# Attention with a norm, then a gated convolution FFN: the norm factor of two batches carried to all lanes by transfers through DRAM

## The chip, the cores and the metric

The kernel runs on one core of one Trainium2 chip. A core has a matrix engine (PE, with its weight loads shown apart as PEld), a vector engine (DVE), a scalar engine (ACT), a general engine (POOL) and a queue engine (SP) that here does nothing but issue transfers. Matmul results land in eight banks of an on-chip accumulator memory (`banks` in the program); everything else that the engines touch lies in SBUF, on 128 partitions ("lanes"). The inputs and the output lie in DRAM. Each engine works its own instructions strictly in order; engines wait for each other, and for transfers, on semaphores. The metric is the device time of one execution in microseconds (us), lower is better.

## The reference

```python
kv  = einsum('bhsd,bhse->bhde', k, v)          # 8 batches, 8 heads, 576 rows, 64 columns
o   = einsum('bhsd,bhde->bhse', q, kv)
rms = sqrt(mean(o * o, axis=-1) + 1e-6)        # over the 64 columns of one head and row
x   = o / rms * g_norm                         # heads side by side: [8, 576, 512]
h   = maximum(x @ w_in, 0)                     # [8, 576, 1024]
c   = conv over rows, 3 taps, one weight per column and tap
out = (h * sigmoid(c)) @ w_out                 # [8, 576, 512]
```

The part of interest is the factor 1/rms. There is one number per batch, head and row, and it multiplies the 64 columns of that head.

## The kernel before

Everything is computed transposed: the 512 columns of `x` lie on the partitions, as four tiles of 128 (two heads to a tile), and the 576 rows lie along the free axis. Work on a batch is cut by `u` (tiles 0 and 1, or 2 and 3) and by `s` (two parts of the rows; for batches 6 and 7 these are 320 and 256 columns wide). A piece is called (b, u, s) below.

The whole program is one long written order, the string `ORDER` (lines 59 to 135). Each token is an operation, its arguments, and after `@` the slots of the buffers that it takes; lines 779 to 784 run the tokens, and lines 786 to 794 chain every engine's instructions in exactly that order. So nothing is rescheduled: an engine that has to wait holds up all that stands behind it on that engine, and SP's transfers are issued in the order of their tokens.

For batches 4 and 5 together, and again for 6 and 7 together, the norm is done so:

- `ox` (L491) makes a piece of `o` in two banks; `oc` (L518) copies it to SBUF as `o32` in fp32, and `sq` (L506) squares it, both on ACT.
- `ss` (L560) sums the squares over the 64 columns with PE, against a 0/1 matrix `sel`. The sums of both batches end in one bank, one sum to a lane: lane 32 t + 2 c + i holds tile t, head i of that tile, and c = 2 (b - b0) + s.
- `ln` (L571) turns them into factors on ACT: `rs`, 128 lanes by 320 columns, fp32 (its activation is L574).
- `sl` (L577) splits `rs` on DVE into bf16 parts `wparts` (four instructions, L581 to L584). Each factor lies on three lanes, and each lane keeps another part (high, middle, low).
- `sp` (L587) spreads a factor over the 64 lanes of its head: two matmuls for each piece against the 0/1 matrix `spread` (L593), which add the three parts up again in fp32 in two banks.
- `mu` (L598) multiplies on DVE: `x = o32 * g * spread factor`, one instruction for each piece (L599).

Then `hs` (L624, matmuls L628; one half of the rows of one tile f of `h`) and `hm` (L608, L613; a whole batch) make `h` from `x` and `w_in`. `rh` and `re` (L633, L618) apply the relu on ACT. `ta`, `aa`, `ab` (L678 to L692) make the convolution on DVE, `sg` (L695) the sigmoid on ACT, `mg` (L720) the gate product on DVE. `om` (L727, L732) is the product with `w_out`, four tiles f at a time; `ea` and `ed` (ACT, DVE) copy its result to SBUF, and `st` (L746, transfer L748) issues the store from SP.

Around the change the order is this. `ln.6`, then on DVE `sl.6`, then six pieces: `mu.6.1.1`, `mu.6.0.1`, `mu.7.0.0`, `mu.7.1.0`, `mu.7.1.1`, `mu.7.0.1`; behind them `mg.4.2.2`, the convolution of two tiles of batches 4 and 5, `mg.4.2.3`, and then `mu.6.0.0` and `mu.6.1.0`. PE has the six `sp` in two groups around the eight matmuls of `om.1.5`, then the eight of `om.1.3`, then `hs.7.6.0`, which reads (7, 0, 0) and (7, 1, 0), then `hs.7.6.1`, which reads (7, 1, 1) and (7, 0, 1), and from there `hs` and `hm` without another product to put between. The last two `sp` stand about 7 us further on. On SP there are the stores `st.1.2` and `st.0.5` in this stretch, then `st.1.3` and `st.1.1`.

Of the kernel before, what the change touches and what calls it, by code (L numbers as in the profile page):

```python
# [109 lines left out]
sq.7.0.0@3 om.1.2.4.4 ea.1.2@1 om.1.8.4.4 ea.1.8@3 ox.7.1.1@6 sq.7.1.1@4 ox.7.0.1@0 sq.7.0.1@5 ox.7.1.0@2 sq.7.1.0@7  # L110
oc.7.0.1@7 om.1.1.0.4@4 om.1.1.4.4 ss.6.6.2@5 ss.7.6.2 ln.6@0 oc.7.1.1@2 st.1.0 st.1.8 ea.1.1@4 oc.7.1.0@3
om.1.4.0.4@0 om.1.4.4.4 ea.1.4@2 om.1.7.0.4@1 ta.4.2.7@1 ta.4.2.6 aa.4.2.3 ab.4.2.3 om.1.7.4.4 ea.1.7@3 ta.4.2.5
aa.4.2.2 ab.4.2.2 sg.4.2.4 sg.4.2.5 sg.4.2.7 sl.6@1 sp.6.1.1.6@6 mu.6.1.1@0 sp.6.0.1.6@4 mu.6.0.1 sp.7.0.0.6@2
mu.7.0.0@2 st.1.2 st.0.5 om.1.5.0.4@0 om.1.5.4.4 sp.7.1.0.6@6 mu.7.1.0 sp.7.0.1.6@4 sp.7.1.1.6@2 om.1.3.0.4@1
om.1.3.4.4 ea.1.3@1 st.1.3 st.1.1 hs.7.6.0@6 rh.7.6.0@1 mu.7.1.1 mu.7.0.1 hs.7.6.1@7 hs.7.4.0@2 hs.7.2.1@1 rh.7.4.0
rh.7.6.1 rh.7.2.1 hs.7.5.0@3 rh.7.5.0 ea.1.5@0 sg.4.2.6 hs.6.7.1@2 rh.6.7.1 hm.4.2@4 hs.6.0.1@3 rh.6.0.1 hs.6.6.1@0
rh.6.6.1 re.4.2 hm.4.3@6 re.4.3 hs.7.0.0@1 mg.4.2.2 hs.7.1.1@0 rh.7.1.1 ta.4.2.1@0 ta.4.2.0 aa.4.2.0 mg.4.2.3 ab.4.2.0
sg.4.2.0 sp.6.0.0.6@2 mu.6.0.0 sp.6.1.0.6@4 mu.6.1.0 hs.7.2.0@6 rh.7.2.0 sg.4.2.1 hs.7.3.0@0 hs.7.5.1@7 rh.7.3.0
ta.4.2.3@1 ta.4.2.2 aa.4.2.1 ab.4.2.1 rh.7.0.0 mg.4.2.0 st.1.5 hs.6.3.1@2 hs.6.2.1@3 hs.6.4.0@6 hs.6.7.0@4 rh.6.4.0
rh.6.7.0 hs.6.4.1@0 rh.6.4.1 hs.6.3.0@1 rh.6.3.1 rh.6.3.0 hs.6.1.1@5 rh.6.1.1 rh.6.2.1 hs.6.5.1@0 rh.6.5.1 ta.6.1.4@0  # L120
hs.6.6.0@2 rh.6.6.0 hs.6.5.0@1 rh.6.5.0 ta.6.1.5 hs.6.0.0@3 aa.6.1.2 sg.4.2.2 hs.7.4.1@0 hs.7.7.1@1 sg.4.2.3 rh.7.7.1
# [17 lines left out]
def kernel(  # L139
# [20 lines left out]
    NT = D_model // P  # L160
# [71 lines left out]
    GW = 320 if TQ else HS  # L232
    HEAD = (("sync", "q.0.0 k.0.1 k.1.1 q.1.0 k.2.1 k.3.1 q.0.1 q.1.1"), ("scalar", "v.0.2 v.2.2"))

    def cols(b, s):
        if b == 0:
            return tuple(r * D for r in RS[s])
        if b in TQ:
            return s * 5 * D, (5 + s * 4) * D
        return s * HS, (s + 1) * HS  # L240

    def width(b, s):
        c0, c1 = cols(b, s)
        return c1 - c0

    @op
    def pre():
        T["stg"] = ring("h", [P, 2, NT, R * D], FP32, "stg")
        T["stq"] = ring("h", [P, NT, R * D], FP32, "stq")
        for name, head in HEAD:  # L250
            queue = getattr(nc, name)
            for what in head.split():
                x, t, s = what.split(".")
                t, s = int(t), int(s)
                if x == "q":
# [9 lines left out]
        nc.vector.memset(zero, 0.0)
# [92 lines left out]
    @op  # L358
    def Li(f0, n):
        at = slice(f0 * P, (f0 + n) * P)  # L360
        nc.gpsimd.dma_start(out=w_in_sb[:, :, at], in_=moe_w_in[:, at].rearrange("(t p) f -> p t f", p=P))

    @op
    def Lo(f0, n):
# [41 lines left out]
                            start=(r == 0), stop=(r == R - 1))  # L406

    def kvc(eng, b, u0, n):
        if u0 == 0:
            T["kvb", b] = ring("kvb", [P, 2, 2 * D], BF16, "kvb")  # L410
        at = slice(u0 * D, (u0 + n) * D)
        to, fr = T["kvb", b][:, :, at], T["kv", b, u0][:, :, at]
        if eng:
            nc.vector.tensor_copy(to, fr)
        else:
            nc.scalar.activation(to, fr, AX.Copy)

    @op
    def kva(b, u0, n): kvc(0, b, u0, n)

    @op
    def kvd(b, u0, n): kvc(1, b, u0, n)
# [12 lines left out]
                        qkv["q", b][half(i), 2 * u + tt, r * D:(r + 1) * D], ident[half(i), half(i)])  # L435

    def qc(eng, b, u, s):
        if s == 0:
            T["qT", b, u] = ring("qT", [P, 2, S], BF16, "qT")
        c0, c1 = cols(b, s) if b == 0 else (0, S)  # L440
        to, fr = T["qT", b, u][:, :, c0:c1], T["qt", b, u, s][:, :, c0:c1]
        if eng:
            nc.vector.tensor_copy(to, fr)  # L443
        else:
            nc.scalar.activation(to, fr, AX.Copy)

# [150 lines left out]
    @op  # L597
    def mu(b, u, s):  # L598
        nc.vector.scalar_tensor_tensor(  # L599
            x_part(b, u, s), T["o32", b, u, s], g_sb, T["sp", b, u, s], op0=AL.mult, op1=AL.mult)  # L600
# [178 lines left out]
    for token in ORDER.split():  # L779
        what, _, at = token.partition("@")  # L780
# [44 lines left out]
```

## Time and profile before

| | |
|---|---|
| Time, median of 3 runs | 177.79 us (177.78 to 178.52) |
| Span of the profiled execution | 175.6 us, 5070 instructions |
| PE busy | 167.9 us (96%) |
| DVE busy | 149.5 us (85%) |
| ACT busy | 148.9 us (85%) |
| Mean transfer rate over the span | 166 GB/s |

The profile is of one execution, and its times start at the first instruction. The times of the runs take in a little more than that span: 177.79 against 175.6 us, 2.2 us. The views used below are: the page's summary; the chain of work that ended last, in order of time; the timeline of one engine, in which a row is a run of like instructions (start, duration of the whole run, engine, line, operation, output <- inputs, shapes, count, and in brackets the idle time ahead of it with what ended it); the answer about one line or a group of transfers, with the time from issue to landing; and a table of stretches of time with the busy time of each engine in each. "SPq" rows are the issue of a transfer, not the transfer itself. Matmuls overlap in their pipeline, so the duration of one matmul (some 0.3 us) is not its spacing.

### The profile page before, as it was taken

To read this page: it belongs to the slowest core of one execution; us is meant where nothing else is said; L and a number is where in the kernel's file an instruction comes from. 1 tells how busy PE (TensorE), PEld (TensorE's weight loads), DVE (VectorE), ACT (ScalarE), POOL (GpSimd) and SP (SyncE) were. 2 spreads that over 40 slices of the span, in tenths; PEclk is the share of its full clock that TensorE was granted. 3 is DMA by queue.
4 is the path that set the end of the run, shared out by engine and by line. 5 is a ranking of instruction groups with operands and counts; after the bars stand their busy time and mean duration, and the time that the engine had idled before them with its cause. 6 is when DMAs were issued, how large, how long until landed. Compare 5 with 4: busy or idle time off the path is not lost.

```text
span 175.6 us, 5070 instructions
## 1 busy us (share of the span) xinstructions
PE 167.9 (96%) x2097; PEld 100.0 (57%) x2114; DVE 149.5 (85%) x290; ACT 148.9 (85%) x268; POOL 22.2 (13%) x35
## 2 busy tenths in 40 slices
PE   7979999999999999999999999999999999999992
PEld 2334766676447677644467764444877744444451
DVE  2796638899688899999999998989999999999950
ACT  2368899999978999999999998999999967676721
POOL 3094512200603013030000000000000000000000
PEclk9999999999999999999999999999999999999999
DMA  5999999999999999999999050330310003064486
GB/s 159 392 323 207 207 207 207 208 208 209 207 241 230 227 207 207 170 182 197 258 181 161 14 134 0 119 123 0 119 63 0 0 0 116 13 239 175 179 304 237
DMA packets 25911, 29.11 MB, mean 166 GB/s; under 512 B 6036, under 2 KB 20384, under 8 KB 25888
## 3 DMA queue, kind: packets, MB, share of 16 engines
q0 software_dynamic: 13296, 14.50, 49.2%
q1 hardware_dynamic: 12048, 13.11, 26.2%
q10 hardware_dynamic: 544, 1.18, 1.7%
q8 instruction: 16, 0.26, 0.6%
q14 instruction: 7, 0.06, 0.1%
HBM read 32.52 MB, written 9.44 MB: 239 GB/s over the span
## 4 chain that ended last, share of the span: by engine, by line
PE 76%; DVE 12%; ACT 5%; DMA 3%; issue 3%; ACTq 0%; DVEq 0%
PE banks L732 32%; PE banks L628 14%; PE banks L613 9%; PE banks L658 4%; DMA stg<-in_v_dram 3%; PE banks L460 3%; DVE h L722 2%; PE banks L708 2%; ACT taps L698 2%; PE banks L402 2%; PE banks L593 2%; PE banks L433 1%; PE banks L528 1%; DVE taps L681 1%; PE banks L286 1%
## 5 line engine op out<-in xcount | busy, mean ns | idle before, releaser
L732 PE MATMUL banks<-w_out_sb,h 128*128 128x512 bf16 x267 | 62.8, 379 | 1.2 <-issue 0.6
L698 ACT ACTIVATE taps<-taps,cw 128x576 bf16<-128x576 bf16 (+1 forms) x44 | 40.6, 958 | 5.7 <-DVE taps L692 5.5
L732 PEld LDWEIGHTS <-h 128*128 128x128 bf16 x280 | 26.2, 98 | 30.0 <-issue 1.1
L628 PE MATMUL banks<-x,w_in_sb 128*128 128x288 bf16 (+2 forms) x256 | 34.2, 286 | 0.0
L640 ACT ACTIVATE h<-banks 128x288 bf16<-128x288 f32 (+2 forms) x80 | 29.5, 460 | 0.3 <-PE banks L658 0.2
L628 PEld LDWEIGHTS <-w_in_sb 128*128 128x128 bf16 x256 | 24.4, 98 | 7.8 <-issue 0.8
L722 DVE TENSOR_TENSOR h<-h,taps 128x1152 bf16<-128x1152 bf16 (+1 forms) x24 | 22.8, 952 | 1.2 <-ACT taps L698 1.2
L687 DVE TENSOR_TENSOR taps<-taps 128x1152 bf16<-128x1152 bf16 (+1 forms) x22 | 21.5, 978 | 0.5
L509 ACT ACTIVATE sq<-banks 128x576 bf16<-128x576 f32 (+2 forms) x32 | 20.8, 691 | 1.1 <-PE banks L460 1.1
L692 DVE TENSOR_TENSOR taps<-taps,h 128x1152 bf16<-128x1152 bf16 (+1 forms) x22 | 21.4, 972 | 0.3
L681 DVE TENSOR_SCALAR taps<-h,cw 128x576 bf16<-128x576 bf16 (+1 forms) x44 | 18.7, 424 | 0.6 <-ACT h L665 0.5
L682 DVE TENSOR_SCALAR taps<-h,cw 128x576 bf16<-128x576 bf16 (+1 forms) x44 | 18.4, 418 | 0.0
L738 ACT ACTIVATE row<-banks 128x512 f32<-128x512 f32 x23 | 13.5, 597 | 5.7 <-PE banks L732 4.2
L658 PE MATMUL banks<-x,w_in_sb 128*128 128x288 bf16 (+2 forms) x128 | 17.7, 286 | 0.1
L613 PE MATMUL banks<-x,w_in_sb 128*128 128x288 bf16 x128 | 16.9, 286 | 0.0
L556 DVE SCALAR_TENSOR_TENSOR x<-banks,cw,rs 128x576 bf16<-128x576 f32 (+2 forms) x16 | 13.0, 816 | 3.9 <-ACT rs L545 3.6
L658 PEld LDWEIGHTS <-w_in_sb 128*128 128x128 bf16 x128 | 12.0, 98 | 4.4 <-issue 0.5
L227 ACT ACT_TABLE_LOAD x10 | 12.8, 1283 | 2.0 <-issue 1.8
L613 PEld LDWEIGHTS <-w_in_sb 128*128 128x128 bf16 x128 | 12.3, 98 | 3.7 <-issue 0.2
L443 DVE COPY qT<-banks 128x1152 bf16<-128x1152 bf16 (+2 forms) x13 | 8.8, 681 | 5.7 <-PE banks L433 5.7
L545 ACT ACTIVATE rs<-banks,eps_sb 128x576 f32<-128x576 f32 (+2 forms) x16 | 11.8, 740 | 1.1 <-PE banks L528 1.1
L599 DVE SCALAR_TENSOR_TENSOR x<-o,cw,banks 128x576 bf16<-128x576 f32 (+2 forms) x16 | 12.1, 810 | 0.7 <-PE banks L593 0.5
(89 smaller groups left out, 162.9 us busy)
## 6 DMA issues: line engine op xcount, KB each, us to landing
out_dram<-row SPq DMA_DIRECT2D x35, 256.0 KB, 2.3
q_sb<-in_q_dram POOLq DMA_DIRECT2D x6, 576.0 KB, 17.9
k_sb<-in_k_dram POOLq DMA_DIRECT2D x6, 576.0 KB, 14.5
v_sb<-in_v_dram POOLq DMA_DIRECT2D x6, 576.0 KB, 17.9
stg<-in_v_dram ACTq DMA_DIRECT2D x2, 576.0 KB, 6.2
stg<-in_k_dram SPq DMA_DIRECT2D x4, 288.0 KB, 6.9
w_in_sb<-in_moe_w_in_dram POOLq DMA_DIRECT2D x2, 512.0 KB, 9.9
w_out_sb<-in_moe_w_out_dram POOLq DMA_DIRECT2D x1, 1024.0 KB, 15.5
```

The costliest lines, as they stand in the source:

```text
L509: nc.scalar.activation(T["sq", b, u, s], T["o", b, u, s], AX.Square)
L613: nc.tensor.matmul(ps[:, s, :HS], w_in_sb[:, t, f * P:(f + 1) * P], T["x", b][:, t, c0:c1], start=(t == 0), stop=(t == NT - 1))
L628: nc.tensor.matmul(ps, w_in_sb[:, t, f * P:(f + 1) * P], T["x", b][:, t, c0:c1], start=(t == 0), stop=(t == NT - 1))
L640: nc.scalar.activation(h, fr, AX.Relu)
L658: nc.tensor.matmul(T[at], w_in_sb[:, t, f * P:(f + 1) * P], T["x", b][:, t, c0:c1], start=(t == 0), stop=(t == NT - 1))
L681: nc.vector.tensor_scalar_mul(tap[:, 0, f % 2, :n, 8:8 + S], h[:, f], cw[:, f:f + 1])
L682: nc.vector.tensor_scalar_mul(tap[:, 1, f % 2, :n, :S], h[:, f], cw[:, 2 * NF + f:2 * NF + f + 1])
L687: nc.vector.tensor_add(tap[:, 1, :, :n, :S], tap[:, 0, :, :n, 7:7 + S], tap[:, 1, :, :n, 1:1 + S])
L692: nc.vector.tensor_add(y, y, span(b, n)[:, 2 * j:2 * j + 2])
L698: nc.scalar.activation(y, y, AX.Sigmoid, scale=cw[:, NF + f:NF + f + 1])
L722: nc.vector.tensor_mul(h, h, tap_of(b, j)[:, 1, :, :n, :S])
L732: nc.tensor.matmul(T["om", p, m], h[:, f, m * P:(m + 1) * P], w_out_sb[:, f, :], start=(f == 0), stop=(f == NF - 1))
```

## The change

For batches 6 and 7 alone, `sl.6` and the eight `sp` are taken out. In the place of `sl.6` stands `dw.6`: SP writes `rs` (128 lanes by 320 columns, fp32, 164 KB) to a scratch tensor `rd` in DRAM. In the place of each `sp` stands a `df`: two transfers from SP, one to each half of the lanes, which read two rows of `rd` (one factor row for each tile of the piece) and write each of them to 64 lanes. The target is an fp32 tile `spread` in SBUF, laid into buffers that held `q`, `k` or `v` of earlier batches. `mu` is the same instruction; it reads the factor from SBUF now, not from the banks. The places in the order are the same, and batches 4 and 5 keep the split and the products.

So SP issues 17 transfers more: one, then six (for three pieces), then, behind `st.1.2` and `st.0.5`, six more, and, behind `st.1.3` and `st.1.1`, four. PE has 16 matmuls and 16 weight loads fewer, DVE four instructions fewer. The buffer `k` slot 0 is used twice, for (6, 0, 1) and then for (7, 1, 1), so the second transfer waits for `mu.6.0.1`.

The diff also defines operations for loading `w_in` in another way (`w` in `pre`, `wd`, `wa`), and lets `kvc` and `qc` make their tile at any first call; the order uses none of that.

```diff
-aa.4.2.2 ab.4.2.2 sg.4.2.4 sg.4.2.5 sg.4.2.7 sl.6@1 sp.6.1.1.6@6 mu.6.1.1@0 sp.6.0.1.6@4 mu.6.0.1 sp.7.0.0.6@2
-mu.7.0.0@2 st.1.2 st.0.5 om.1.5.0.4@0 om.1.5.4.4 sp.7.1.0.6@6 mu.7.1.0 sp.7.0.1.6@4 sp.7.1.1.6@2 om.1.3.0.4@1
+aa.4.2.2 ab.4.2.2 sg.4.2.4 sg.4.2.5 sg.4.2.7 dw.6 df.6.1.1.6@1 mu.6.1.1@0 df.6.0.1.6@0 mu.6.0.1 df.7.0.0.6@1
+mu.7.0.0@2 st.1.2 st.0.5 om.1.5.0.4@0 om.1.5.4.4 df.7.1.0.6@2 mu.7.1.0 df.7.0.1.6@1 df.7.1.1.6@0 om.1.3.0.4@1
 om.1.3.4.4 ea.1.3@1 st.1.3 st.1.1 hs.7.6.0@6 rh.7.6.0@1 mu.7.1.1 mu.7.0.1 hs.7.6.1@7 hs.7.4.0@2 hs.7.2.1@1 rh.7.4.0
 rh.7.6.1 rh.7.2.1 hs.7.5.0@3 rh.7.5.0 ea.1.5@0 sg.4.2.6 hs.6.7.1@2 rh.6.7.1 hm.4.2@4 hs.6.0.1@3 rh.6.0.1 hs.6.6.1@0
 rh.6.6.1 re.4.2 hm.4.3@6 re.4.3 hs.7.0.0@1 mg.4.2.2 hs.7.1.1@0 rh.7.1.1 ta.4.2.1@0 ta.4.2.0 aa.4.2.0 mg.4.2.3 ab.4.2.0
-sg.4.2.0 sp.6.0.0.6@2 mu.6.0.0 sp.6.1.0.6@4 mu.6.1.0 hs.7.2.0@6 rh.7.2.0 sg.4.2.1 hs.7.3.0@0 hs.7.5.1@7 rh.7.3.0
+sg.4.2.0 df.6.0.0.6@0 mu.6.0.0 df.6.1.0.6@0 mu.6.1.0 hs.7.2.0@6 rh.7.2.0 sg.4.2.1 hs.7.3.0@0 hs.7.5.1@7 rh.7.3.0
...
+    dram = pool("dram", 1, space=bass.MemoryType.DRAM)
...
+    @op
+    def dw(b0):
+        T["rd", b0] = dram.tile([P, GW], FP32, name="rd")
+        nc.sync.dma_start(out=T["rd", b0], in_=T["rs", b0])
+
+    @op
+    def df(b, u, s, b0):
+        w, c = width(b, s), 2 * (b - b0) + s
+        to = T["sp", b, u, s] = ring("qkv"[(4 * (b - b0) + 2 * u + s) % 3], [P, 2, 320], FP32, "spread")[:, :, :w]
+        fr = T["rd", b0].rearrange("(t c i) w -> c i t w", t=NT, i=2)[c, :, 2 * u:2 * u + 2, :w]
+        for i in range(2):
+            nc.sync.dma_start(out=to[half(i)], in_=fr[i].unsqueeze(0).to_broadcast([D, 2, w]))
```

More of the change, by code (lines that the diff above doesn't have):

```diff
@@ L244, in width @@
         return c1 - c0
+    w_rows = moe_w_in.rearrange("(t p) f -> p t f", p=P)
     @op
@@ L254, in pre @@
                 t, s = int(t), int(s)
-                if x == "q":
+                if x == "w":
+                    T["stw", t] = ring("x", [P, NT, s * P], FP32, "stw")
+                    queue.dma_start(out=T["stw", t], in_=w_rows[:, :, t * P:(t + s) * P])
+                elif x == "q":
                     ts, (c0, c1) = slice(2 * t, 2 * t + 2), cols(0, s)
@@ L360, in Li, with wd, wa @@
         at = slice(f0 * P, (f0 + n) * P)
-        nc.gpsimd.dma_start(out=w_in_sb[:, :, at], in_=moe_w_in[:, at].rearrange("(t p) f -> p t f", p=P))
+        nc.gpsimd.dma_start(out=w_in_sb[:, :, at], in_=w_rows[:, :, at])
+    @op
+    def wd(f0, n):
+        nc.vector.tensor_copy(w_in_sb[:, :, f0 * P:(f0 + n) * P], T["stw", f0])
+    @op
+    def wa(f0, n):
+        nc.scalar.activation(w_in_sb[:, :, f0 * P:(f0 + n) * P], T["stw", f0], AX.Copy)
     @op
@@ L408, in kvc @@
     def kvc(eng, b, u0, n):
-        if u0 == 0:
+        if ("kvb", b) not in T:
             T["kvb", b] = ring("kvb", [P, 2, 2 * D], BF16, "kvb")
@@ L437, in qc @@
     def qc(eng, b, u, s):
-        if s == 0:
+        if ("qT", b, u) not in T:
             T["qT", b, u] = ring("qT", [P, 2, S], BF16, "qT")
@@ L600, in mu @@
             x_part(b, u, s), T["o32", b, u, s], g_sb, T["sp", b, u, s], op0=AL.mult, op1=AL.mult)
+    @op
+    def dw(b0):
+        T["rd", b0] = dram.tile([P, GW], FP32, name="rd")
+        nc.sync.dma_start(out=T["rd", b0], in_=T["rs", b0])
+    @op
+    def df(b, u, s, b0):
[4 more added lines that the diff above has]
+            nc.sync.dma_start(out=to[half(i)], in_=fr[i].unsqueeze(0).to_broadcast([D, 2, w]))
     def h_of(b, f):
```

## The prediction

> **What bounds the kernel now.** I read the page's summary first, then the chain that ended last, then stretches, then the timelines of PE and DVE around the change, and SP's last.
>
> ```profile
> span 175.6 us, 5070 instructions
> GB/s 159 392 323 207 207 207 207 208 208 209 207 241 230 227 207 207 170 182 197 258 181 161 14 134 0 119 123 0 119 63 0 0 0 116 13 239 175 179 304 237
> PE 76%; DVE 12%; ACT 5%; DMA 3%; issue 3%; ACTq 0%; DVEq 0%
> ```
>
> The chain is PE for 76% of the span. An average hides where, so here is the chain in order of time (start, duration, what), from the change on:
>
> ```profile
> 118.22 0.34 PE banks L593 x4
> 119.28 1.54 DVE x L599 x2
> 120.86 0.28 PE banks L593 x2
> ...
> 122.98 2.94 PE banks L628 x24
> ...
> 129.98 11.11 PE banks L628 x88
> ...
> 141.35 10.74 PE banks L732 x49
> ...
> 172.27 0.38 ACT row L767
> ```
>
> From 122.98 to 172.27 the chain is matmuls, with no wait that another engine ends: 24 in 2.94 us is 0.1225 us each, 49 in 10.74 is 0.219 each. PE has no room there, so a delay of PE at 123 us comes out at the end. Only the stretch before shows another engine (two `mu`). The stretches (us of the stretch, then busy of PE, PEld, DVE, ACT, POOL, granted clock, DMA share, GB/s):
>
> ```profile
> 118.00:123.00 5.00, 4.82 (x31) 1.96 (x31) 4.55 (x8) 4.97 (x6) 0.00 (x0) 1.00 0.00 0
> 130.00:140.00 10.00, 10.00 (x81) 7.80 (x82) 9.90 (x16) 9.94 (x21) 0.00 (x0) 1.00 0.01 2
> ```
>
> DVE is full as well (9.90 of 10.00), so a delay of DVE is not caught up either. No bytes move from 118 to 123: the new transfers have the queues to themselves.
>
> **The change: what goes.** PE, then DVE, then the activation that makes `rs`, then two single `mu`:
>
> ```profile
> 118.22 0.42 PE L593 MATMUL banks<-wparts,spread 32*128 32x256 bf16 x6
> 118.58 1.90 PE L732 MATMUL banks<-w_out_sb,h 128*128 128x512 bf16 x8
> 120.41 0.74 PE L593 MATMUL banks<-wparts,spread 32*128 32x320 bf16 x6
> 121.08 1.90 PE L732 MATMUL banks<-w_out_sb,h 128*128 128x512 bf16 x8
> 122.82 3.10 PE L628 MATMUL banks<-x,w_in_sb 128*128 128x320 bf16 x24
> 129.67 0.31 PE L593 MATMUL banks<-wparts,spread 32*128 32x320 bf16 x4
> ...
> 114.66 1.36 DVE L692 TENSOR_TENSOR taps<-taps,h 128x2304 bf16<-128x2304 bf16 x1
> 116.30 0.33 DVE L581 CAST hi<-rs 128x320 bf16<-128x320 f32 x1 [0.28 <-ACT rs L574]
> 117.61 0.55 DVE L584 SCALAR_TENSOR_TENSOR wparts<-hi,nb,rs 128x320 bf16<-128x320 bf16 x1
> 118.61 4.35 DVE L599 SCALAR_TENSOR_TENSOR x<-o,cw,banks 128x512 bf16<-128x512 f32 x6 [0.45 <-PE banks L593]
> 122.88 1.35 DVE L722 TENSOR_TENSOR h<-h,taps 128x2304 bf16<-128x2304 bf16 x1
> 127.67 1.36 DVE L722 TENSOR_TENSOR h<-h,taps 128x2304 bf16<-128x2304 bf16 x1 [0.32 <-ACT taps L698]
> ...
> 115.74 0.53 ACT L574 ACTIVATE rs<-banks,eps_sb 128x320 f32<-128x320 f32 x1
> ...
> 120.76 0.88 DVE L599 SCALAR_TENSOR_TENSOR x<-o,cw,banks 128x640 bf16<-128x640 f32 x1
> ...
> 122.22 0.74 DVE L599 SCALAR_TENSOR_TENSOR x<-o,cw,banks 128x512 bf16<-128x512 f32 x1
> ```
>
> PE loses the 16 `sp` matmuls: 118.58 - 118.22 = 0.36, 121.08 - 120.41 = 0.67, and 0.3 at 129.67; 1.3 us. The first two let `om.1.5` and `om.1.3` run earlier, so PE is through them at 122.82 - 1.03 = 121.8. DVE loses `sl.6`, 116.30 to 118.16, 1.9 us, but it gains nothing by that: `mu` is next and now waits for transfers. `mu` keeps its price: the factor comes from SBUF in place of the banks, and `sl`'s instruction of the same kind with both inputs in SBUF takes 0.55 us for 320 columns against 0.74 for 512, so I see no discount (bounds: 0.1 us either way for each, 0.6 in six).
>
> **What comes, on SP.** No row shows a transfer that reads DRAM into 64 lanes. The nearest: `kvx` (64 lanes, SBUF to SBUF), the stores (SBUF to DRAM), and the first loads:
>
> ```profile
> 99.23 0.46 SPq L489 DMA_DIRECT2D kvx<-kvb  x1
> ...
> 99.74 0.59 SPq L489 DMA_DIRECT2D kvx<-kvb  x1
> ...
> 100.38 0.58 SPq L748 DMA_DIRECT2D out_dram<-row  x1
> ...
> DMA to landing us min/median/max: 1.8/1.8/1.9
> ...
> 124.24 0.33 SPq L748 DMA_DIRECT2D out_dram<-row  x1
> ...
> 124.61 0.43 SPq L748 DMA_DIRECT2D out_dram<-row  x1
> ...
> DMA to landing us min/median/max: 1.9/2.2/2.5
> ...
> stq<-in_q_dram SPq DMA_DIRECT2D x2, 256.0 KB, 5.7
> ```
>
> The first landing row is of the two `kvx` at 99 us, the second of the two 128 KB stores at the end. Issues on SP follow one another: 99.23, 99.74, 100.38 is one each 0.5 to 0.64 us, the two stores one each 0.38 to 0.48. I take 0.6 for a `df` transfer (nearest in shape), with 0.42 and 0.65 as ends, and 0.85 for `st.1.2` with `st.0.5`. For issue to landing I take 2.0 (ends 1.75 and 3; the 5.7 of the first loads was beside a rate of up to 392 GB/s). A pair writes 128 lanes x 2 rows x 256 or 320 fp32 numbers; six pairs carry 4 x 262 + 2 x 328 KB = 1.70 MB in the some 8 us of their issue; at the 207 GB/s of the long load phase that takes 8.2 us, so bandwidth is about even with the issues and I add nothing.
>
> - `rs` is there at 115.74 + 0.53 = 116.27. `dw.6` issues at 116.3 and lands at 118.3. Everything behind it on SP waits, stores included; they have time.
> - `df` number k (0 to 11) issues at 118.35 + 0.6 k, plus 0.85 from k = 6 on. A pair is there 2.0 us after its second issue: 120.95 for (6,1,1), 122.15 for (6,0,1), 123.35 for (7,0,0), 125.4 for (7,1,0), 126.6 for (7,0,1), 127.8 for (7,1,1). The last pair's buffer is free long before, after `mu.6.0.1` at 122.9.
> - DVE is free from 116.02 and stands until 120.95, then runs each `mu` as its pair lands. `mu.7.1.0` ends at 125.4 + 0.05 + 0.88 = 126.3, `mu.7.1.1` starts at 127.85, `mu.7.0.1` 0.7 later (six in 4.35 us before) and ends at 129.3. Before it ended at 122.22 + 0.74 = 122.96: DVE is 6.3 us late.
> - PE stands from 121.8 to 126.3, does `hs.7.6.0` (four matmuls of 320 columns, 0.54 us by 0.1225 for a mean of 288), and stands again until 129.3 for `hs.7.6.1`, which before started at 122.82 + 0.54 = 123.36: PE is 5.94 late, and 5.64 after the 0.3 of the last two `sp`.
> - The last four `df`, behind two more stores, issue by 129 and land by 131; `mu.6.0.0` stands at 130.2 + 6 on DVE. Nothing: the queue on DVE covers them, with 5 us to spare.
> - ACT meanwhile has its sigmoids and copies; `sg.4.2.6` behind PE's `hs.7.5.0` slides with PE, so `mg.4.2.3` moves from 127.67 by the larger of PE's 5.94 and DVE's 6.3 - 0.32: 5.97 late.
>
> At the end the two delays meet again (DVE's last gate product, and the matmuls in the window of its first reader; `om.3.7.4.4` is the second of the two, at 166.82):
>
> ```profile
> 165.91 0.75 DVE L722 TENSOR_TENSOR h<-h,taps 128x1152 bf16<-128x1152 bf16 x1
> ...
> 166.61 0.59 PE L732 MATMUL banks<-w_out_sb,h 128*128 128x512 bf16 x2
> ```
>
> The product ends at 166.66, 0.16 us ahead of its reader. So the end is late by the larger of 5.64 and 5.97 - 0.16 = 5.8. Span 175.6 + 5.8 = 181.4; with the 2.2 us around it (the median 177.79 less the span) 183.6.
>
> The Trainium skill ("DMA: Bandwidth & Descriptors", Anatomy of one DMA) gives a transfer about 2.0 us fixed, most of it waiting for the write to be confirmed, plus its bytes at 436 GB/s. It speaks against this change, which puts two such waits in a row where 2.3 us of split and product stood. By it `dw` and each `df` land after 2.0 + 0.4 us, 0.8 later in all, and the time would be 184.4. The rows of this trace (1.9 to 2.5 us for 128 KB) agree as far as they go; that fit is for the other way of issuing.
>
> **The rivals.**
>
> *The stall also halves the PE clock.* The first fillers ran slow and the next fast, and the idle tail kept the full clock:
>
> ```profile
> 1.20 4.45 PE L286 MATMUL banks<-zero 128*128 128x512 bf16 x10 [1.20 <-DVE zero L265]
> 5.83 2.12 PE L286 MATMUL banks<-zero 128*128 128x512 bf16 x9
> ...
> 172.30:175.60 3.30, 0.00 (x0) 0.00 (x0) 0.00 (x0) 0.36 (x1) 0.00 (x0) 1.00 0.53 188
> ```
>
> Ten matmuls took 4.45 us from idle; at the later 2.12 / 9 they would take 2.36, so a cold start costs 2.1 us. Against: 3.3 us of idle at the end left the granted clock at 1.00. For: here PE stands 4.5 us, works 0.5, and stands 2.4 more. PE late by 5.64 + 2.1, and DVE by about as much through `sg.4.2.6`: 185.6. The Trainium skill ("TensorE: Matmul & The Clock Gate", Part 1) says that an idle window of about 3.4 us, free-running, drops the clock to half, and a busy one brings it back; by that rule the 4.5 us hold a whole window in one third of the phases, more if the 0.5 us between count as idle. The trace bears it out at the start only.
>
> *The transfers are slower than their issue.* Each reads two rows of at most 1280 bytes 64 times over; no row shows such reads. At half of 207 GB/s the 1.70 MB take 16.4 us, 8 more than I allow, and the time would be 191. Against: nothing else moves then.
>
> *Not slower.* The round trip fits into what stood there. For that `mu.7.0.1` must be through by 123.36 + 0.3, so the last pair must land by 122.3, its second issue be out by 120.3, 1.95 us after the first: 0.15 us for each of the 13 steps from issue to issue, two stores among them. The shortest issue row is 0.33. If it did fit, the 1.3 us of PE are left and the time would be 176.5.
>
> **How the numbers follow.** Stall with the clock kept, 183.6: 0.50. Stall with half clock, 185.6: 0.27. Slow transfers, 187 to 193: 0.13. A shorter chain (issues at 0.42, landings at 1.75, `dw` at 1.9: the last `mu` at 126.9, PE 3.6 late, 181.4, less with cheaper `mu`): 0.06. Not slower: 0.04, half of it a gain. With the last few of the slow ones and the last case left out the range is 180.9 to 188.5; the likeliest case alone has 181.4 to 185. About 0.5% (0.9 us) can be told from no change. Slower 0.96, same 0.02, faster 0.02.
>
> **What would show it.** DVE idle from 116.0 to about 121 before the first `mu`, ended by a transfer, and gaps of 0.5 us and more between the six; PE idle about 4.5 and 2.4 us ahead of and behind one `hs`; SP issuing `df` each 0.6 us; the last `mu` of the six at about 129.3; the end 5.8 late with no new idle of PE behind 130. The forecast is wrong if a `df` pair takes far other than 2.6 us from its first issue, if the granted clock drops after the stall, or if PE shows idle ahead of `om` at the end.

## The result and the profile after

| | before | after |
|---|---|---|
| Time, median | 177.81 us | 188.88 us |
| Ratio | | 1.062 (95%: 1.060 to 1.064) |
| Span of the profiled execution | 175.6 us | 187.0 us |
| PE busy, share of the span | 96% | 91% |
| Mean granted clock of PE | 1.00 | 0.973 |

The kernel is 11.1 us slower. The forecast was 183.6 us with a range up to 188.5: the sign was right, the size was not, and the time lies 0.4 us outside the range. Two lines of the page's slices show the place (40 slices of 4.7 us each; busy tenths of PE, then the granted clock in tenths):

```profile
PE   7889999999999999999999999912599999999992
PEclk9999999999999999999999999995589999999999
```

One hole in PE, at slices 27 to 29, and from its second slice on three with a lower clock (0.5, 0.5 and 0.8). The rest is as full as before. The timeline of DVE, the six `mu` (L613):

```profile
122.55 0.75 DVE L613 SCALAR_TENSOR_TENSOR x<-o,cw,spread 128x512 bf16<-128x512 f32 x1 [6.45 <-DMA spread<-rd]
124.58 0.75 DVE L613 SCALAR_TENSOR_TENSOR x<-o,cw,spread 128x512 bf16<-128x512 f32 x1 [1.29 <-DMA spread<-rd]
125.89 0.88 DVE L613 SCALAR_TENSOR_TENSOR x<-o,cw,spread 128x640 bf16<-128x640 f32 x1 [0.55 <-DMA spread<-rd]
128.92 0.88 DVE L613 SCALAR_TENSOR_TENSOR x<-o,cw,spread 128x640 bf16<-128x640 f32 x1 [2.15 <-DMA spread<-rd]
131.40 1.41 DVE L613 SCALAR_TENSOR_TENSOR x<-o,cw,spread 128x512 bf16<-128x512 f32 x2 [1.59 <-DMA spread<-rd]
```

Each `mu` is held by a transfer, and the last of the six ends at 131.40 + 1.41 = 132.81; the forecast had 129.3. PE's timeline (L759 is `om`, L655 `hs`):

```profile
118.46 3.61 PE L759 MATMUL banks<-w_out_sb,h 128*128 128x512 bf16 x16 [0.18 <-ACT row L765]
126.83 0.65 PE L655 MATMUL banks<-x,w_in_sb 128*128 128x320 bf16 x2 [4.75 <-DVE x L613]
129.86 0.69 PE L655 MATMUL banks<-x,w_in_sb 128*128 128x320 bf16 x2 [2.39 <-DVE x L613]
132.87 4.64 PE L655 MATMUL banks<-x,w_in_sb 128*128 128x256 bf16 x20 [2.32 <-DVE x L613]
```

PE stands three times (4.75, 2.39 and 2.32 us), not twice: `hs.7.6.0` reads two pieces, so its matmuls fall into two pairs. `hs.7.6.1` starts at 132.87 against 123.36 before (by the prediction's working), 9.5 us late; less the 0.3 us of the last two `sp` that is 9.2. Then 20 matmuls take 4.64 us, 0.23 each, where the forecast went by 0.1225: another 2 us. Together 11.2, and 177.8 + 11.2 = 189.0 is the time to 0.1 us. The chain of the last-ending work and the stretches confirm that nothing more was lost behind it:

```profile
116.38 1.76 DMA rd<-rs
...
121.76 4.01 DMA spread<-rd
...
127.18 4.13 DMA spread<-rd
...
152.43 29.35 PE banks L759 x136
```

```profile
123.00:130.00 7.00, 0.79 (x3) 0.35 (x3) 2.81 (x4) 1.42 (x2) 0.00 (x0) 0.78 0.77 244
130.00:140.00 10.00, 7.68 (x45) 5.21 (x44) 6.75 (x9) 4.93 (x11) 0.00 (x0) 0.64 0.55 151
140.00:150.00 10.00, 9.96 (x82) 7.76 (x81) 9.93 (x15) 9.68 (x21) 0.00 (x0) 1.00 0.01 2
```

In the chain, transfers stand where two `mu` stood, and three of them come to 9.9 us; `om` at the end starts at 152.43, 11.1 us later than the 141.35 of before. In the stretches (columns as before) PE works 0.79 of 7 us between 123 and 130, the clock is 0.64 between 130 and 140, and from 140 to 150 PE is full at full clock; the chain behind that is PE's matmuls up to the last copy.

### The profile page after: what moved, and what is told of

Its sections match the earlier page's. It is cut to its first block, busy times and chain, and to the rows that moved or that the text cites. A ratio compares the mean times of both kernels' runs of the same rounds, so it can differ in the third digit from the quotient of the medians.

```text
span 187.0 us, 5080 instructions
## 1 busy us (share of the span) xinstructions
PE 170.7 (91%) x2098; PEld 100.6 (54%) x2098; DVE 147.9 (79%) x286; ACT 149.2 (80%) x268; POOL 22.2 (12%) x35
## 4 chain that ended last, share of the span: by engine, by line
PE 79%; DMA 8%; DVE 5%; ACT 3%; SPq 2%; issue 1%; DVEq 0%; ACTq 0%
PE banks L759 28%; PE banks L655 18%; PE banks L640 9%; PE banks L685 7%; DMA spread<-rd 4%; DMA stg<-in_v_dram 3%; PE banks L474 3%; PE banks L447 2%; PE banks L416 2%; SPq L627 2%; PE banks L292 2%; PE banks L735 2%; PE banks L542 2%; PE banks L607 1%; PE banks L784 1%
## 5 line engine op out<-in xcount | busy, mean ns | idle before, releaser
L759 PE MATMUL banks<-w_out_sb,h 128*128 128x512 bf16 x280 | 64.3, 379 | 0.2 <-ACT row L765 0.2
L655 PE MATMUL banks<-x,w_in_sb 128*128 128x288 bf16 (+2 forms) x256 | 36.9, 299 | 9.5 <-DVE x L613 9.5
L759 PEld LDWEIGHTS <-h 128*128 128x128 bf16 x280 | 26.3, 98 | 30.5 <-issue 1.3
L655 PEld LDWEIGHTS <-w_in_sb 128*128 128x128 bf16 x256 | 25.5, 101 | 19.2 <-issue 11.3
L685 PE MATMUL banks<-x,w_in_sb 128*128 128x288 bf16 (+2 forms) x128 | 17.7, 286 | 0.0
L613 DVE SCALAR_TENSOR_TENSOR x<-o,cw,spread 128x512 bf16<-128x512 f32 (+1 forms) x8 | 6.4, 816 | 12.0 <-DMA spread<-rd 12.0
L685 PEld LDWEIGHTS <-w_in_sb 128*128 128x128 bf16 x128 | 12.0, 98 | 4.4 <-issue 0.5
L640 PEld LDWEIGHTS <-w_in_sb 128*128 128x128 bf16 x128 | 12.3, 98 | 3.7 <-issue 0.2
```

The lines of the kernel that those rows point to most:

```text
L640: nc.tensor.matmul(ps[:, s, :HS], w_in_sb[:, t, f * P:(f + 1) * P], T["x", b][:, t, c0:c1], start=(t == 0), stop=(t == NT - 1))
L655: nc.tensor.matmul(ps, w_in_sb[:, t, f * P:(f + 1) * P], T["x", b][:, t, c0:c1], start=(t == 0), stop=(t == NT - 1))
L685: nc.tensor.matmul(T[at], w_in_sb[:, t, f * P:(f + 1) * P], T["x", b][:, t, c0:c1], start=(t == 0), stop=(t == NT - 1))
L759: nc.tensor.matmul(T["om", p, m], h[:, f, m * P:(m + 1) * P], w_out_sb[:, f, :], start=(f == 0), stop=(f == NF - 1))
```

## The experiments

All are compared with the kernel before on the same chip (177.6 to 177.7 us). The changed kernel's own kernel before took 177.81 us, so where a run is set against the changed kernel's 188.88, the difference of the two losses stands in brackets: it is 0.1 to 0.3 us smaller. They are told by question: the transfers, the clock, the work removed, and what it takes to hide the waits.

### The transfers: why 4 us and not 2?

SP's rows of the changed kernel, then the time to landing of the answers about L627, cut to the first pair, the fourth and the last of the six:

```profile
116.38 0.33 SPq L619 DMA_DIRECT2D rd<-rs  x1
118.28 4.08 SPq L627 DMA_DIRECT2D spread<-rd  x6
122.41 1.06 SPq L775 DMA_DIRECT2D out_dram<-row  x2
123.56 4.22 SPq L627 DMA_DIRECT2D spread<-rd  x6
```

```profile
L627 SPq DMA_DIRECT2D spread<-rd x2: 600/630/660, 118.3 to 119.0; - x2
DMA to landing us min/median/max: 3.5/3.5/3.5
...
L627 SPq DMA_DIRECT2D spread<-rd x2: 585/762/938, 123.6 to 124.2; - x2
DMA to landing us min/median/max: 4.6/4.6/4.6
...
L627 SPq DMA_DIRECT2D spread<-rd x2: 573/590/606, 126.6 to 127.2; - x2
DMA to landing us min/median/max: 4.1/4.2/4.3
```

An issue of the twelve takes 0.57 to 0.66 us (one 0.94), but no landing is under 3.5. (The last four, which nothing needs for some time, land after 5.9 to 6.8.) Three causes were possible: a read from DRAM into 64 lanes is slow by itself; the same row read 64 times is slow; the transfers crowd each other.

**Transfers alone.** Into the kernel before, behind `st.1.5`, five transfers were put that nothing reads, each done before the next is issued: 64 lanes of 2 x 256 numbers from different rows, the same from one and the same row, both again with 2 x 320, and 128 lanes of 2 x 256 from different rows.

```diff
-... mg.4.2.0 st.1.5 hs.6.3.1@2 ...
+... mg.4.2.0 st.1.5 pd.256@1 pb.256 pd.320 pb.320 pf.256 hs.6.3.1@2 ...
```

> The kernel before, with five transfers added on SP behind st.1.5, where its queues are quiet; each writes the same unused tile, so each waits for the one ahead and is seen alone. In order: 64 lanes x 2 rows of 256 fp32 from 64 different places of q; the same shape with the same two rows for all lanes; the two again with 320 columns; and 128 lanes x 2 rows of 256 from different places. Theory A (reading the same rows 64 times is what is slow): 2.2 us from issue to landing with different rows, 3.5 with the same rows. Rival B (any transfer from DRAM into 64 lanes takes so long): 3.5 for all four. Rival C (only the crowd of transfers is slow): 2.2 for all four. The time stays at 177.8, since nothing waits for the tile.

The answers about the line of these transfers, one by one in that order:

```profile
DMA to landing us min/median/max: 2.7/2.7/2.7
...
DMA to landing us min/median/max: 3.3/3.3/3.3
...
DMA to landing us min/median/max: 2.9/2.9/2.9
...
DMA to landing us min/median/max: 3.4/3.4/3.4
...
DMA to landing us min/median/max: 3.2/3.2/3.2
```

The kernel took 178.05 us in one execution. Alone, the read lands after 2.7 to 2.9 us where the forecast took 2.0; one row read 64 times adds 0.5 to 0.6; the 3.5 to 4.6 of the series are 0.2 to 1.2 more again. So all three have a part. For the last transfer of the six pieces, which sets the end, the 4.1 us are 2.1 above the forecast, and by these rows that is 0.7 for a read from DRAM, 0.6 for the one row and 0.8 for the series: none of them is most of it. The forecast's 2.0 came from stores and copies, which landed after 1.8 to 2.5 us.

**Different rows in the series.** All `df` but the first transfer read 64 different rows of `q`, so the norm of batches 6 and 7 is left out.

```diff
-            nc.sync.dma_start(out=to[half(i)], in_=fr[i].unsqueeze(0).to_broadcast([D, 2, w]))
+            at = (4 * c + 2 * u + i) * 320
+            first = (b, u, s, i) == (6, 1, 1, 0)
+            nc.sync.dma_start(
+                out=to[half(i)],
+                in_=fr[i].unsqueeze(0).to_broadcast([D, 2, w]) if first else own[:, :, at:at + w])
```

> The changed kernel, but all transfers of the factor except the very first read 64 different places of q in place of the same two rows of the scratch tensor; sizes, lanes, count and issue order are the same. Batches 6 and 7 are multiplied by numbers of q, so their norm is left out. Theory A (same rows): landings fall from 4.1 to some 2.3 us, the last of the six products ends about 1.9 us earlier, and the time is 187.0 with the half clock still there, 185 if the shorter stall keeps the clock. Rivals B and C (shape, or the crowd): landings stay at about 4 and the time at 188.9.

187.52 us (187.34 to 187.7), 1.36 less than the changed kernel (1.1). The answer about the first eleven of these transfers and DVE's last of the six `mu`:

```profile
DMA to landing us min/median/max: 3.3/3.8/4.0
```

```profile
130.12 1.42 DVE L613 SCALAR_TENSOR_TENSOR x<-o,cw,spread 128x512 bf16<-128x512 f32 x2 [1.12 <-DMA spread<-in_q_dram]
```

The six end at 131.54 in place of 132.81, 1.3 earlier, and the time follows. That is what reading one row 64 times costs here, 1.1 to 1.4 us. (The run reads `q` in place of the fresh scratch tensor, too, and does not tell that apart; the lone transfers, all from `q`, give 0.5 to 0.6 for the row.) It is a small part of the 11 us, and even different rows land 3.8 us after issue in the median.

**The stores out of the way.** The four stores go behind all sixteen `df`, with row buffers of their own for the two copies that would wait for them.

```diff
-mu.7.0.0@2 st.1.2 st.0.5 om.1.5.0.4@0 ... ea.1.3@1 st.1.3 st.1.1 hs.7.6.0@6 ... ea.1.5@0 ...
+mu.7.0.0@2 om.1.5.0.4@0 ... ea.1.3@6 hs.7.6.0@6 ... ea.1.5@7 ...
-sg.4.2.0 df.6.0.0.6@0 mu.6.0.0 df.6.1.0.6@0 mu.6.1.0 hs.7.2.0@6
+sg.4.2.0 df.6.0.0.6@0 mu.6.0.0 df.6.1.0.6@0 mu.6.1.0 st.1.2 st.0.5 st.1.3 st.1.1 hs.7.2.0@6
```

> The changed kernel with the four stores st.1.2, st.0.5, st.1.3, st.1.1 moved on SP behind all the factor's transfers, and two row buffers more so that the copies ea.1.3 and ea.1.5 need not wait for them. Theory (SP's issue sets the pace; the two stores ahead of the fourth pair take 1.15 us of it): the fourth to sixth pair land 1.1 us earlier, the last of the six products ends at 131.7 in place of 132.8, and the time is 187.7 with the half clock. Rival (the pace is set by the transfer engines, whose packets are slow): the pairs land at most 0.5 earlier, time 188.5.

187.51 us (186.97 to 188.04), as expected. SP's row of the sixteen, their time to landing, and DVE's last two of the six `mu`:

```profile
118.20 11.21 SPq L627 DMA_DIRECT2D spread<-rd  x16
...
DMA to landing us min/median/max: 3.4/4.4/5.0
...
130.42 1.41 DVE L613 SCALAR_TENSOR_TENSOR x<-o,cw,spread 128x512 bf16<-128x512 f32 x2 [1.81 <-DMA spread<-rd]
```

Without the two stores the queue goes through in 0.70 us a transfer. The twelve for the six pieces land after 3.4 to 4.6 us, as in the changed kernel (3.5 to 4.6). The last `mu` ends at 131.83 in place of 132.81, and the time is 1.4 us shorter (1.2): at this pace the issue on SP still sets when a piece is there.

**Two queues.** The second half of each pair is issued from POOL.

```diff
-            nc.sync.dma_start(out=to[half(i)], in_=fr[i].unsqueeze(0).to_broadcast([D, 2, w]))
+            (nc.gpsimd if i else nc.sync).dma_start(out=to[half(i)], in_=fr[i].unsqueeze(0).to_broadcast([D, 2, w]))
```

> The changed kernel with the second transfer of each pair issued from POOL's queue, so that a pair costs SP 0.62 us in place of 1.3. Theory (SP's issue sets the pace): the sixth pair is issued 3.5 us earlier, the last product ends some 3 us earlier, time 186. Rival (the transfer engines set the pace, or POOL's own issue is slower than 0.6 us): the last product ends at 132 or later, time 188.5 or more.

188.61 us (188.34 to 188.88): no gain that two executions can show. The time to landing of the sixteen, the stretch of the second half of the six, and POOL's second row of issues:

```profile
DMA to landing us min/median/max: 3.5/5.9/7.5
```

```profile
123.00:130.00 7.00, 0.69 (x2) 0.25 (x2) 2.37 (x4) 1.38 (x2) 1.79 (x3) 0.71 1.06 277
```

```profile
126.24 1.90 POOL L627 DMA_DIRECT2D spread<-rd  x3 [4.57 <-DVE x L613]
```

What is issued earlier takes longer: the median goes from 4.1 to 5.9 us. The last transfer of the fifth pair is issued at 122.4 in place of 125.9 and lands after 7.5 us in place of 4.0, at 129.9 in both kernels. The transfer engines' share (1.06 by the profile's count, next to last in the row) shows them full. So they carry the first five pairs no faster than one queue issues them, and the remark in the forecast that bandwidth is about even with the issues held, but its conclusion "add nothing" did not: two even limits in a row make a queue. The Trainium skill ("DMA: Bandwidth & Descriptors", Issuing engines are not separate DMA queues) says that transfers started by different engines run on the same transfer engines, and that starting them from several saves only the time of the issue. The first five pairs agree: issued up to 3.5 us earlier, they landed no more than 0.2 us earlier.

The sixth pair, which sets the end, is no test of the queues, because it was hardly issued earlier. It takes the buffer of (6, 0, 1), so POOL waits 4.57 us for `mu.6.0.1` and issues its half at 126.24, where SP issued that half at 127.18. The same with a buffer of its own was not run.

**The transfers without the wait.** The kernel with the stores behind, all transfers issued and landing, but `mu` of batches 6 and 7 reads `o` in the factor's place.

```diff
-            x_part(b, u, s), T["o32", b, u, s], g_sb, T["sp", b, u, s], op0=AL.mult, op1=AL.mult)
+            x_part(b, u, s), T["o32", b, u, s], g_sb, T["o32" if b > 5 else "sp", b, u, s],
+            op0=AL.mult, op1=AL.mult)
```

> The kernel with the four stores behind all df (187.5 us), with every transfer still issued and landing, but with mu multiplying o by itself in batches 6 and 7, so that nothing waits for a transfer but the stores behind them on SP; the factor of these two batches is left out. If the transfers cost only by being waited for, this takes 177.5, as the kernel with neither transfers nor split (177.51). If the transfers also slow the engines by their traffic (SBUF, DRAM or the issue on SP), it takes more, by what they cost: 179 or above would show that.

177.60 us (177.52 to 177.71), ratio 0.9998 (0.9989 to 1.0007). SP's row and the same stretch:

```profile
118.21 10.65 SPq L628 DMA_DIRECT2D spread<-rd  x16
```

```profile
123.00:130.00 7.00, 6.25 (x51) 4.81 (x50) 6.49 (x8) 6.90 (x15) 0.00 (x0) 1.00 0.86 198
```

The same transfers go through in nearly the same time (10.65 us for the sixteen issues, 11.21 there), and there is no loss. PE, DVE and ACT are busy 6.25, 6.49 and 6.90 us of the 7; in the kernel without any of these transfers (under "The work removed") they are 6.24, 6.49 and 6.89. So the transfers' traffic and issue slow no engine here; all that they cost, they cost by being waited for. Between this kernel and the one with the stores behind lies only who reads `spread`: 9.9 us, the half clock included.

### The clock

**Fillers ahead of the two `hs`.** PE gets matmuls of zeros while it would stand: 18 ahead of `hs.7.6.0`, 9 ahead of `hs.7.6.1`.

```diff
-om.1.3.4.4 ea.1.3@1 st.1.3 st.1.1 hs.7.6.0@6 rh.7.6.0@1 mu.7.1.1 mu.7.0.1 hs.7.6.1@7
+om.1.3.4.4 ea.1.3@1 st.1.3 st.1.1 fi.18.512@5 hs.7.6.0@6 rh.7.6.0@1 mu.7.1.1 mu.7.0.1 fi.9.512@5 hs.7.6.1@7
```

> The changed kernel with 27 dummy matmuls on a free bank: 18 ahead of hs.7.6.0 and 9 ahead of hs.7.6.1, 0.216 us each, so that PE does not stand during the waits for the transfers. Theory (the stall halves the PE clock from 126.9 to 137.1 us, and that costs some 2 us on its own): the granted clock stays 1.00, the first 20 hs matmuls behind the stall take 2.5 us in place of 4.64, and the time is 187.2 (bound then by DVE, whose six products end 9.9 late), 1.7 below the changed kernel. Rival (the half clock is hidden behind the wait of DVE): clock 1.00 but the time stays at 188.9.

188.52 us (187.83 and 189.22): nothing told apart. PE's timeline shows why (L292 are the fillers):

```profile
121.85 4.05 PE L292 MATMUL banks<-zero 128*128 128x512 bf16 x18
126.65 0.43 PE L655 MATMUL banks<-x,w_in_sb 128*128 128x320 bf16 x2 [0.75 <-DVE x L613]
129.85 0.69 PE L655 MATMUL banks<-x,w_in_sb 128*128 128x320 bf16 x2 [2.76 <-DVE x L613]
130.33 4.04 PE L292 MATMUL banks<-zero 128*128 128x512 bf16 x9
```

The plan of this run overlooked that `hs.7.6.0` waits twice. The wait in its middle, 2.76 us behind 0.43 us of work, was not filled, and the clock fell in it: the next nine fillers take 0.45 us each where the first eighteen took 0.22, and they ran past the time when `mu` was ready.

**Fillers in all three waits.** `hs.7.6.0` is written in two halves (`hk`), with eight fillers between and eight behind.

```diff
-... hs.7.6.0@6 rh.7.6.0@1 mu.7.1.1 mu.7.0.1 hs.7.6.1@7
+... fi.18.512@5 hk.7.6.0.0@6 fi.8.512@5 hk.7.6.0.1 rh.7.6.0@1 mu.7.1.1 mu.7.0.1 fi.8.512@5 hs.7.6.1@7
```

> The first try with dummy matmuls left PE standing 2.8 us between the two halves of hs.7.6.0 (tiles 0 and 1 wait for one product, tiles 2 and 3 for another), and the clock still fell, at 129.0. Here hs.7.6.0 is cut into its halves with 18 dummy matmuls ahead of the first, 8 between and 8 ahead of hs.7.6.1. Theory (the half clock adds some 2 us of its own): granted clock 1.00 throughout, the 20 hs matmuls behind the stall take 2.5 us, the end is then bound by DVE, time 187.0. Rival (the half clock is hidden behind DVE's own delay): clock 1.00, time 188.9.

186.97 us (186.6 to 187.67), and the granted clock is 1.00 throughout. The twenty matmuls that took 4.64 us:

```profile
132.64 2.56 PE L655 MATMUL banks<-x,w_in_sb 128*128 128x256 bf16 x20 [0.50 <-DVE x L613]
```

They start at 132.64, as late as before, and take 2.56. So the half clock cost 1.9 us (188.88 - 186.97; 1.8 by the losses, 2.08 by the rows), and it came from the stall, as that rival said. With the clock kept, the chain runs over DVE and ACT from 132.6 to 142.8 us before it is PE's again.

By the granted clock in the traces, it is half from 126.9 to 137.1 us in the changed kernel, right behind the wait of 4.75 us, and from 129.0 to 135.8 in the first run with fillers, where in the 3.4 us before the drop PE had worked some 0.7 us. The Trainium skill ("TensorE: Matmul & The Clock Gate", Part 1) gives a free-running window of about 3.4 us for it. The two traces agree with that: the half clock lasted 10.2 and 6.8 us, three and two such windows. By that window, 0.7 us of work in it did not count as busy.

### The work removed

`dw` and all `df` are taken out, and `mu` reads `o` in the factor's place as above (the norm of batches 6 and 7 is left out), in the order of the changed kernel. What is left is the change without its transfers.

```diff
-... sg.4.2.7 dw.6 df.6.1.1.6@1 mu.6.1.1@0 df.6.0.1.6@0 mu.6.0.1 df.7.0.0.6@1 mu.7.0.0@2 ...
+... sg.4.2.7 mu.6.1.1@0 mu.6.0.1 mu.7.0.0@2 ...
```

> The changed kernel without the transfers: dw.6 and all df are out, and mu of batches 6 and 7 multiplies o by itself, so their norm factor is left out. It shows what the removal of the split and the products is worth when nothing takes their place. Theory: PE gains 1.0 us ahead of hs.7.6.0 and 0.3 later and is the bound, so the time is 176.5. Rival (the removed work was beside other work): 177.8.

177.51 us, ratio 0.9995 (0.9984 to 1.0006): the 1.9 us of `sl.6` on DVE and the 1.3 us of PE's products are worth nothing at the end. The chain of this kernel, around the place, and PE's timeline there:

```profile
120.31 3.55 ACT taps L726 x3
123.86 0.48 ACT row L766
124.34 1.73 ACT h L668 x5
...
133.54 7.56 PE banks L656 x60
```

```profile
124.39 1.58 PE L656 MATMUL banks<-x,w_in_sb 128*128 128x256 bf16 x12 [0.76 <-ACT row L766]
```

With the norm out of the way, ACT's sigmoids and its copy of `om.1.3` come last, and PE stands 0.76 us for a bank. PE was the bound in the chain of before, but ACT was right behind it.

### Can the waits be covered?

**A new order.** The transfers are issued in a row, PE is given `hm.4.2`, `hm.4.3` and eight `hs` of (6, s = 1) ahead of those that need the late pieces, and DVE has parts of the convolution and `mg` between the `mu`.

```diff
+... df.6.1.1.6@1 df.6.0.1.6@0 df.7.0.0.6@1 df.7.1.0.6@2 df.7.0.1.6@1 om.1.5.0.4@0 ... hm.4.2@4 re.4.2 hm.4.3@6 re.4.3
+mu.6.1.1@0 mg.4.2.2 mu.6.0.1 df.7.1.1.6@0 ... hs.6.7.1@2 rh.6.7.1@1 ... hs.6.5.1@5 rh.6.5.1 mu.7.0.0@2 ta.4.2.1@0 mu.7.1.0 ta.4.2.0
+hs.7.6.0@6 rh.7.6.0 ... mu.7.0.1 mu.7.1.1 aa.4.2.0 mg.4.2.3 ab.4.2.0 sg.4.2.0
```

> The changed kernel with another order around the transfers and the same work: all transfers are issued back to back, the stores behind them; PE does hm.4.2, hm.4.3 and the eight hs of (batch 6, s=1), which need the first two pieces alone, ahead of any hs of batch 7; DVE does mg.4.2.2, ta.4.2.1 and ta.4.2.0 between the products as the pieces land. Theory (the loss is the uncovered wait, and there are some 5.5 us of PE work and 2.3 of DVE work to put under it): PE stands 1.5 us at most, the clock stays 1.00, DVE stands 6.4 us ahead of its first product and stays some 4.8 us late, time 182.4. Rival (the transfers themselves disturb the other engines, or ACT becomes the bound): above 185.

185.35 us (184.9 to 186.06), some 3 more than expected. One row of PE's timeline tells it:

```profile
139.42 10.11 PE L657 MATMUL banks<-x,w_in_sb 128*128 128x320 bf16 x56 [5.15 <-ACT h L669]
```

This order has `sg.4.2.0` ahead of relus on ACT. It waits for the convolution, the relus behind it keep their banks, and PE stands 5.15 us; the clock fell once more (0.978 in the mean).

**The same with the sigmoids behind the relus.** The `hs` of batch 7 also stand in a somewhat other sequence.

```diff
-hs.7.6.0@6 rh.7.6.0 ... mu.7.0.1 mu.7.1.1 aa.4.2.0 mg.4.2.3 ab.4.2.0 sg.4.2.0
+mu.7.0.1 mu.7.1.1 aa.4.2.0 mg.4.2.3 ab.4.2.0 mu.6.0.0 mu.6.1.0
+hs.7.6.0@6 rh.7.6.0 ... hs.7.5.1@7 sg.4.2.0 sg.4.2.1 ta.4.2.3@1 ...
```

> As e9, but with the two convolution buffers of the changed kernel, so that DVE has nothing to do from 116.0 until its first product at 122.5, and with the sigmoids behind all relus of batch 7; this is e8 without the wait of ACT that its order made. Theory: PE's stall is 1.2 us and ACT's are gone, but DVE stays some 4.8 us late, time 182.4. Rival (DVE's delay is caught up, PE alone counts): 179.

181.97 us (181.53 to 182.57), ratio 1.025 (1.022 to 1.028), as expected. Of the 11.1 us, 6.9 are gone (6.7), with every transfer still there.

**DVE filled as well.** A third buffer for the convolution lets DVE do two of its tiles ahead of the first `mu`. Behind that the order on DVE changes too: `mg.4.2.3` and the next two tiles of the convolution stand among the last four `mu` and ahead of `mu.6.0.0`, which the cut shown leaves out.

```diff
-df.7.0.1.6@1  om.1.5.0.4@0
+df.7.0.1.6@1 ta.4.2.1@2 ta.4.2.0 aa.4.2.0 ab.4.2.0 om.1.5.0.4@0
-    taps = [consts.tile([P, 2, 2, 2, TW], BF16, name=f"taps{i}") for i in range(2)]
+    taps = [consts.tile([P, 2, 2, 2, TW], BF16, name=f"taps{i}") for i in range(3)]
```

> The changed kernel with all the cover that can be put under the wait: the order of e8 on SP and PE, a third buffer for the convolution so that DVE can do ta.4.2.1, ta.4.2.0, aa.4.2.0 and ab.4.2.0 (4.5 us) ahead of its first product, and ACT's sigmoids of tiles 0 and 1 placed behind the relus of batch 6 so that ACT does not wait for DVE. Theory (the loss was nothing but the uncovered wait and the clock it costs; the work that went out is beside ACT and gains nothing): PE stands 1.2 us ahead of the hs of batch 6, the clock stays 1.00, DVE is through its six products at 131.4 but with most of its other work done, time 178.3. Rival (the transfers cost the engines something besides the wait): 181 or more.

181.51 us in the median of six (180.04 to 181.75), ratio 1.023 (1.021 to 1.025): the 178.3 was missed. PE's timeline of an execution of 180.05 us:

```profile
125.12 1.91 PE L657 MATMUL banks<-x,w_in_sb 128*128 128x256 bf16 x16 [1.24 <-DVE x L615]
...
135.73 0.45 PE L657 MATMUL banks<-x,w_in_sb 128*128 128x320 bf16 x2 [1.53 <-DVE x L615]
```

PE still waits for `mu` in two places. Are these waits still the transfers', or are they the order's?

**That order with no transfers at all.** `dw` and `df` out, `mu` reading `o` as above.

```diff
-aa.4.2.2 ab.4.2.2 sg.4.2.4 sg.4.2.5 sg.4.2.7 dw.6 df.6.1.1.6@1 df.6.0.1.6@0 df.7.0.0.6@1 df.7.1.0.6@2
-df.7.0.1.6@1 ta.4.2.1@2 ta.4.2.0 aa.4.2.0 ab.4.2.0 om.1.5.0.4@0
+aa.4.2.2 ab.4.2.2 sg.4.2.4 sg.4.2.5 sg.4.2.7
+ta.4.2.1@2 ta.4.2.0 aa.4.2.0 ab.4.2.0 om.1.5.0.4@0
```

> The order of the reordered kernel with three buffers of taps (181.5 us), with no transfer of the factor at all: dw and every df are out and mu multiplies o by itself in batches 6 and 7, so the factor of these two batches is left out. If what was left of the loss in that kernel (3.9 us) is the order's own, this takes about 181; if it is the waits for transfers that are still there (1.82 us on DVE and 1.24 on PE ahead of the first mu, the late mu.6.0.0 behind df.6.0.0), this takes about 177.6, as the kernel before. I lean to 178.

181.24 us (180.4 to 182.06), ratio 1.022 (1.018 to 1.026). My leaning to 178 was wrong:

```profile
124.70 2.17 PE L658 MATMUL banks<-x,w_in_sb 128*128 128x256 bf16 x16 [0.74 <-DVE x L615]
...
135.80 0.45 PE L658 MATMUL banks<-x,w_in_sb 128*128 128x320 bf16 x2 [1.53 <-DVE x L615]
```

The second wait is the same to 0.01 us without any transfer. In this order the transfers cost nothing that the runs can tell (181.51 with, 181.24 without, executions from 180.0 to 182.1); the 3.7 us that are left are the order's own. In the trace without transfers PE waits 1.53 and 0.35 us for `mu.6.0.0` and `mu.6.1.0`, which stand behind the convolution on DVE, and 0.74 and 0.49 us ahead of that. A part is the clock: the executions whose mean granted clock is 0.996 to 1.00 take 180.0 to 180.1 with the transfers and 180.4 to 180.5 without, and those at 0.987 to 0.991 take 181.4 to 182.1. Why the clock falls in some executions of one kernel and not in others, no run here shows. An order that covers the waits and costs nothing itself was not found. Nor do the runs show a way below 177.6: in the order as given, the work removed is worth nothing even with the transfers free.

## Why the prediction was wrong

- **What bounds the kernel.** Right: a delay of PE at 123 us came out at the end in full; from 140 on PE is full and nothing is caught up.
- **What goes.** `sl.6` was rightly put at no gain. That PE's 1.3 us "are left" if the rest were hidden (176.5 in that rival) was wrong: without transfers the time is 177.51, as ACT comes next. That `mu` keeps its price with the factor in SBUF was right (0.75 and 0.88 us, 0.74 and 0.88 before).
- **`dw`.** Right: issue 116.38 (forecast 116.3), landing after 1.76 us (2.0).
- **The issues.** "0.6 k, plus 0.85" put the twelfth at 125.8; it came at 127.18, 1.4 later. The rows are 0.57 to 0.66 as taken, but from one issue to the next are 0.7 (4.13 us for six, 118.28 to 122.41), and the two stores took 1.15.
- **Issue to landing, the step that failed.** "For issue to landing I take 2.0 (ends 1.75 and 3)." Measured: 3.5 for the first pair, at most 4.6 in the six, 4.1 for the last, all above the upper end; the first pair takes 4.2 us from its first issue, not 2.6. The last pair was late by 2.1 through this, and with the issues its two `mu` end 3.5 late. The rows that I took it from write to DRAM or stay in SBUF; none reads DRAM. The only row of a read that the prediction shows, the first loads with 5.7 us, was set aside for their load, and that it might be slow for being a read was not weighed.
- **The page's rule.** By the Trainium skill's 2.0 us and the bytes ("DMA: Bandwidth & Descriptors", Anatomy of one DMA), each `df` would land after 2.4, and the time would be 184.4; both are estimates from the page. The measurements decide: 2.7 to 2.9 for a lone read of different rows, 3.5 to 4.6 here. The rule was too low as well, if nearer than mine.
- **The clock.** Forecast as a rival at 2.1 us with 0.27; it came, at 1.9 to 2.1. The likeliest case was therefore wrong in two terms: 183.6 + 3.5 + 2.0 = 189.1, against 188.88. That the price of 2.1 fits is partly luck: it was that of ten matmuls at the start, and here it is half of the 4.3 us that PE worked from 132.87 until the clock came back at 137.1. The prediction took slow transfers and the half clock one at a time, and no case of it had both; the upper end of 188.5 came from slow transfers alone. They are not independent: later landings make the stall longer, and the clock fell in the stall.
- **Slow transfers as a rival.** Its cause, one row read 64 times, is real but worth 1.1 to 1.4 us here, not 8; that its time (187 to 193) was met, mostly through other causes, is luck.
- **`hs.7.6.0`** was taken as one piece of work between two stalls; it waits twice, which made three.
- **The last four `df` at nothing**: right. They land at up to 138 us in place of 131, still ahead of `mu.6.0.0` at 141.57.
- **Which engine sets the end.** The prediction's 5.8 was that of the gate product on DVE, 0.16 us above PE's 5.64. Wrong, at little cost: from 132.87 us to the last copy the chain is PE's matmuls, with no gate product in it.
- One wait was not foreseen: `st.1.2` stands behind the `df` on SP, so its row buffer comes free late, and ACT's copy behind it waits:

```profile
126.43 0.60 ACT L765 ACTIVATE row<-banks 128x512 f32<-128x512 f32 x1 [2.61 <-DMA out_dram<-row]
```

PE has no work then that could use the bank, so I read it as costing nothing; it was not tried alone.

## What to carry to other kernels

Price a transfer by a row that goes the same way (read or write of DRAM, lanes, series or alone), and if there is none, put the upper end where the longest row stands, even if another reason for its length is at hand. A transfer that is off the path cost nothing even in a series, as the run with unread transfers shows; put one on the path of the bounding engine, and its time to landing counts in full, and if PE stands for some microseconds, add the price of the half clock to that same case, not to a rival. Before counting a removed instruction as a gain, look which other engine is next behind the bound.

## What the hardware showed that I had not expected

- A lone read from DRAM into 64 lanes lands 2.7 us (2 x 256 numbers a lane) to 2.9 us (2 x 320) after its issue, the write of 164 KB to DRAM after 1.8.
- The same row read into 64 lanes lands 0.5 to 0.6 us later than 64 different rows.
- Two issuing queues moved the first ten transfers of the series no faster: the tenth, issued 3.5 us earlier, landed at 129.9 us in both, and the median from issue to landing was 5.9 us against 4.1.
- A wait of PE of 2.76 us behind 0.43 us of work let the clock fall to half, though 4.05 us of matmuls stood shortly ahead; the half clock lasted 6.8 us there and 10.2 us in the changed kernel.
